# A planned attention-and-GLU kernel: transposing loads by whole chunks behind wv, the first q evicted by two engines, fill units that either half of TensorE may go on with, and all orders planned anew

## The chip, the cores and the metric

The kernel runs on one core of one Trainium2 chip. The metric is the device time of one execution in microseconds (us). Before the change the runs took 654.67 us in the median of three (654.21 to 656.93). The engines are called here as in the profile: PE (TensorE, with PEld for its weight loads), DVE (VectorE), ACT (ScalarE), POOL (GpSimd) and SP (SyncE, which only issues DMAs in this kernel).

## The reference

x is 2048 x 512 in bf16. One branch is attention with 32 heads of 16, without a mask; the other is a gated product of F = 1376 columns. A gate of one number for each row mixes them.

```python
def reference(A_x, A_wqkv, A_wo, B_x, B_w_gate, B_w_up, B_w_down, gate_w):
    x = A_x
    g = _sigmoid((x * gate_w).sum(-1, keepdims=True))
    # _A_ref: qkv = x @ wqkv, in 32 heads of Dh = 16
    scores = jnp.einsum("bhqd,bhkd->bhqk", q, k) * (Dh ** -0.5)
    p = _softmax(scores, axis=-1)
    a = (o of p @ v, heads side by side) @ wo
    # _B_ref
    b = ((x @ w_gate) * (x @ w_up)) @ w_down
    return g * a + (1 - g) * b
```

## The kernel before, in words

**Attention.** The queries are cut into 4 chunks of 512 rows, the heads into 4 blocks of 8, each in two sets of four (s): 32 groups of 4 heads x 512 queries, called quads, done one after the other. For each quad there are 16 steps, one for each 128 keys. TensorE is used as two row halves of 64 rows (r = 0, 1) with four column tiles of 32 each, and every PE operation of the main part (`pe64`) is four matmuls of 64 rows x 512 columns on one half. The two halves work beside each other. Both lie in one PE queue, whose order is fixed when the program is built; an operation of one half that depends on one of the other waits on a semaphore.

A step has four score operations (two on each half), which fill four PSUM banks. Then it goes one of two ways. In an A step ScalarE takes the exponential of the banks, one, two or three at a time (`exp`, L1863), and two P·V operations follow. In a D step DVE makes an approximate exponential by an integer trick (`dpass`, L1896), three shifted copies are made by DVE or GpSimd (`copy`, L1902 and L1903), and eight P·V operations follow. P·V accumulates in bank 7.

**Fill.** All the other matrix products are `_Unit`s: K, Q and V projections, the gate, the u and g products of the GLU, the output products. A unit has n operations on one half (phase 0) and then n on the other half (phase 1), into one bank, and is then evicted by DVE or ACT. They are called fill because they go where attention leaves PE free.

**The planner.** `_Sched` steps through time when the program is built, with costs for each operation, and writes down an order for each engine. At each moment it asks `try_pe`, `try_act`, `try_dve`, `try_pool`, `try_sp`. Which kind of work PE takes next is set by some fifty numbers (`PAR`), most of which are tables with one entry for each 2 us of planned time (`win`). `f_cont` goes on with a unit that was begun, `f_start` begins the next unit of the list `fill`, `f_slice` emits one operation of a unit. Only the orders and the waits that the data need go into the program; the planned times don't.

**The first stage.** `prologue` of `_Hw` (from L2064) is written out by hand. The first chunk of x is loaded in four parts by SP's and ACT's queues, transposed on PE with an identity, and multiplied with the first 128 columns of wq and wk: four products into bank 5 for q, and into banks 4 and 6 for K. q is evicted four times under four masks (`QM`): two by ACT (L2163, L2164), two by DVE (L2170, L2171). K goes out by DVE (L2162, L2165). The other three chunks of x come by transposing loads, four of 512 x 128 to a chunk, on SP's queue (L2071 is the helper `ld` that issues every load of the stage). wv is loaded by ACT's queue once wk and wq have landed. The planner takes over from there with times at which it expects these things (`t0`, `tx` for the chunks of x, `tw` for the weights); from `late0` on, eight loads with the other columns of wk and wq are issued on SP, `wgap` apart.

Of the kernel before, what the change touches and what calls it, by code (L numbers as in the profile page):

```python
# [110 lines left out]
class _Unit:  # L111
    __slots__ = ("name", "n", "slot", "need", "mm", "evac", "due", "ph", "half", "pos", "bank", "first", "okt", "lastop", "edur", "eeng", "eneed")

    def __init__(self, name, n, mm, need, evac, edur=0, slot=0.216, eeng="dve", eneed=()):
        self.name = name
        self.n = n
        self.mm = mm
        self.need = need
        self.evac = evac
        self.edur = edur  # L120
        self.slot = slot
        self.eeng = eeng
        self.eneed = eneed
        self.due = 0.0
        self.ph = 0
        self.half = 0
        self.pos = 0
        self.bank = None
        self.okt = 0.0
        self.lastop = None  # L130
        self.first = None
# [6 lines left out]
class _Sched:  # L138
# [380 lines left out]
    def late(self, i):  # L519
        if i < 8:  # L520
            key = {3: ("wk", True), 7: ("wq", True)}.get(i)
            self.dma(self.now, lambda: self.hw.late_load(i) if self.hw else None, 3.0, (lambda t, o: self.setr(key, t, o)) if key else (lambda t, o: None), 3)
            self.at(self.now + self.par["wgap"], lambda: self.late(i + 1))
# [86 lines left out]
    def f_slice(self, u, r):  # L610
        op = None
        i = u.pos
        start = u.ph == 0 and i == 0
# [7 lines left out]
        u.lastop = op  # L621
        u.pos += 1
# [3 lines left out]
        if u.pos == u.n:  # L626
            end = self.now + 0.385 + max(0.0, u.slot - 0.216)
            if u.ph == 0:
                u.ph, u.half, u.pos = 1, 1 - r, 0
# [3 lines left out]
            else:  # L633
# [7 lines left out]
                self.at(t)  # L641

# [33 lines left out]
    def f_start(self, r):  # L676
# [6 lines left out]
        u = self.fill[self.fnext]  # L683
        if not self.ok(u.need):
            return False
# [3 lines left out]
        self.fnext += 1  # L689
        u.bank = self.bank_get("F")  # L690
        u.half = r
        self.fact.append(u)
# [50 lines left out]
    def pe_phase(self, r):  # L743
# [26 lines left out]
        if self.o_avail <= self.now + 1e-9:  # L770
            n0, n1 = self.nready(vh), self.nready(1 - vh)
            busy = any(u.half == 1 - vh and 0 <= u.pos < u.n and not (u.ph == 1 and u.okt > self.now) for u in self.fact)
# [23 lines left out]
        if r != vh and self.g("v2") > 0 and self.v_job(r):  # L796
            return True
# [722 lines left out]
    def prologue(self):  # L1520
# [10 lines left out]
        self.act_v = t0 + 0.6  # L1531
        self.dve_v = t0 + 1.9
# [4 lines left out]
        self.setr(("k", 0, 0), t0 + 0.6, g("k"))  # L1537
        self.setr(("x0k",), t0, r["k"] + [r["q1"]] if self.hw else None)
        self.setr(("q", 0, 0, 0), t0, g("q"))
        self.setr(("q0b",), t0 + 0.6, g("q0b"))  # L1540
        self.setr(("q", 0, 0, 1), t0 + 2.0, g("q1"))
        self.setr(("qd", 0), t0 + 2.0, g("q1"))
# [18 lines left out]
        if self.hw:  # L1561
            self.clast[(0, 0)] = [r["od"]]
# [3 lines left out]
        self.at(t0 + 0.1, lambda: self.bfree.append(4))  # L1566
        self.at(t0 + 0.6, lambda: self.bfree.append(6))
        self.at(t0 + 2.0, lambda: self.bfree.append(5))
# [99 lines left out]
class _Hw:  # L1668
# [104 lines left out]
    def warm_mm(self, r):  # L1773
        lo, hi = 64 * r, 64 * r + 64
        mms = [(self.ps[32 * cc : 32 * cc + 32, 7, :], self.KT[lo:hi, 0, 0:32], self.QM[lo:hi, 0, 0, :], True, True, cc) for cc in range(4)]
        return self.pe64(r, mms, [self.r["k0"], self.r["q"]])
# [270 lines left out]
    def turn(self):  # L2047
        return self.P.op("pool", lambda g: g.tensor_tensor(self.mask[:], self.mask[:], self.mask[:], ALU.add), [self.r["q"], self.r["q0b"]])
# [15 lines left out]
    def prologue(self):  # L2064
# [11 lines left out]
        d_wk0 = ld("act", self.wk[:, :, 0:128], wcol(512, 640), "dwk0")  # L2076
# [21 lines left out]

        dT = []
        for ch in range(1, 4):  # L2100
# [54 lines left out]
        k0, kr, fq = proj(4, self.wk), proj(6, self.wk), proj(5, self.wq)  # L2155
        oq = None
        for t in range(4):
            oq = pex(lambda pe, t=t: fq(pe, t), [xe[t], d_wq0])
# [3 lines left out]
        e0 = dve(lambda v: v.tensor_copy(self.KT[:, 0, 0:128], self.ps[:, 4, 0:128]), [ok0])  # L2162
        q_a = P.op("act", lambda a: a.activation(self.QM[:, 0, 0, :], self.ps[:, 5, :], ACT.Copy, scale=self.mask[:, 0:1]), [oq, m1])  # L2163
        q_b = P.op("act", lambda a: a.activation(self.QM[:, 0, 2, :], self.ps[:, 5, :], ACT.Copy, scale=self.mask[:, 1:2]), [oq])  # L2164
# [3 lines left out]
        r["q"] = q_a  # L2168
        r["q0b"] = q_b
        q_c = dve(lambda v: v.tensor_scalar(self.QM[:, 0, 1, :], self.ps[:, 5, :], self.mask[:, 2:3], None, ALU.mult), [q_a, q_b])  # L2170
        r["q1"] = dve(lambda v: v.tensor_scalar(self.QM[:, 0, 3, :], self.ps[:, 5, :], self.mask[:, 3:4], None, ALU.mult), [q_c])  # L2171
        r["x0"] = xe[3]
        r["x0all"] = xe
        r["bankops"] = {0: [xe[0]], 1: [xe[1]], 2: [xe[2]], 3: [xe[3]], 4: [e0], 5: [q_c, r["q1"]], 6: [e1]}
        r["od"] = od
        r["ones"] = on
        r["er1"] = er1
# [381 lines left out]
```

## Time and profile before

| | |
|---|---|
| runs | 654.67 us median of 3, 654.21 to 656.93 |
| profiled execution, first to last instruction | 653.9 us, granted TensorE clock 1.000; no time around the span is given for it |
| instructions | 44031 |
| TensorE matmuls | 22842, some half of it busy 644.9 us |
| weight loads | 18026, 339.2 us |
| DVE, ACT, POOL busy | 609.7, 639.9, 534.8 us |
| DMA | 22.65 MB, 35 GB/s in the mean |
| chain that ended last | 94% of the span on PE, 3% on SP's queue, 1% on DMA, 1% on DVE |

The span is cut by engines in the page's first part; the stretches give the same for a part of the span, with the number of instructions that touch it in brackets. In the timeline a row is one instruction or several alike, with start and length; what stands in square brackets is how long the engine had been idle and what ended that. Records of ACT and DVE overlap a little with the next one of the same engine.

### The profile page before, as it was taken

Reading aid. Unit: us, or ns where it says so; the run is one execution under the profiler, and the core shown is the slowest. Engines: PE = TensorE matmul, PEld = TensorE weight load, DVE = VectorE, ACT = ScalarE, POOL = GpSimd, SP = SyncE. Lnnn points to the kernel's source line nnn. Section 1 sums busy time; section 2 is a strip of 40 time slices with the busy share of each in tenths; the row PEclk is TensorE's granted clock in tenths of the full one; section 3 lists DMA queues with packets and bytes.
Section 4 is the critical chain, followed back from the end, with each engine's and each line's share of the span. In section 5 each row is a group of like instructions: output and inputs, shape, how many; then the busy total and the mean of one; then the engine's idle time right before and its main releaser. Section 6 shows DMA issues by size and latency. Waiting matters only on the chain.

```text
span 653.9 us, 44031 instructions
## 1 busy us (share of the span) xinstructions
PE 644.9 (99%) x22842; PEld 339.2 (52%) x18026; DVE 609.7 (93%) x1001; ACT 639.9 (98%) x1001; POOL 534.8 (82%) x590
## 2 busy tenths in 40 slices
PE   8999999999999999999999999999999999999997
PEld 4464555555555545545554555555554555545552
DVE  7889999999998899999999999999999879999995
ACT  7999999999999999999999999999999999999996
POOL 1235889899999578899999798999998977997972
PEclk9999999999999999999999999999999999999999
DMA  7302342002110110101001010100101011010101
GB/s 156 76 13 61 89 110 35 9 12 70 52 42 9 33 33 16 35 5 35 8 20 31 18 41 13 41 10 13 29 8 43 13 30 38 5 44 8 30 7 49
DMA packets 34583, 22.65 MB, mean 35 GB/s; under 512 B 20028, under 2 KB 31132, under 8 KB 34400
## 3 DMA queue, kind: packets, MB, share of 16 engines
q1 hardware_dynamic: 32912, 18.80, 11.7%
q8 instruction: 159, 2.61, 1.7%
q10 hardware_dynamic: 1488, 1.05, 0.5%
q14 instruction: 24, 0.20, 0.1%
HBM read 11.71 MB, written 2.36 MB: 22 GB/s over the span
## 4 chain that ended last, share of the span: by engine, by line
PE 94%; SPq 3%; DVE 1%; DMA 1%; issue 0%; POOLq 0%; ACT 0%
PE ps L1756 75%; PE ps L1741 19%; SPq L2071 3%; DMA xT<-in_A_x_dram 1%; DVE DB L1896 1%; DVE OT L2061 0%; POOLq L88 0%; ACT oc L2033 0%; DVE KT L1911 0%; DVE hT L1937 0%; PE ps L2024 0%; POOLq L83 0%
## 5 line engine op out<-in xcount | busy, mean ns | idle before, releaser
L1756 PE MATMUL ps<-QM,KT 64*32 64x512 bf16 x6956 | 491.5, 377 | 1.5 <-DVE QM L2171 0.6
L1903 POOL INT64_ADD DB<-DB x433 | 400.0, 942 | 79.6 <-DVE DB L1896 33.3
L1863 ACT ACTIVATE PT<-ps 128x512 bf16<-128x512 f32 (+1 forms) x660 | 443.0, 814 | 0.7 <-PE ps L1756 0.3
L1896 DVE TENSOR_SCALAR DB<-ps 128x512 int16<-128x512 f32 (+1 forms) x623 | 404.8, 684 | 26.2 <-PE ps L1756 21.9
L1756 PEld LDWEIGHTS ps<-QM,KT 64*32 64x32 bf16 x6956 | 158.6, 90 | 179.9 <-DVE DB L1896 49.7
L1741 PE MATMUL ps<-DB,Vp 64*17 64x512 bf16 x3092 | 240.1, 376 | 0.0
L1756 PE MATMUL ps<-PT,Vp 64*17 64x512 bf16 x1798 | 201.9, 376 | 0.0
L1756 PE MATMUL ps<-DB,Vp 64*17 64x512 bf16 x1924 | 182.8, 376 | 0.0
L1741 PE MATMUL ps<-QM,KT 64*32 64x512 bf16 x1236 | 118.8, 376 | 0.1
L1756 PE MATMUL ps<-xT,wu 64*32 64x512 bf16 x1376 | 114.3, 377 | 0.0
L1863 ACT ACTIVATE xT<-ps 128x512 bf16<-128x512 f32 (+1 forms) x144 | 112.8, 856 | 0.4 <-PE ps L1756 0.4
L1756 PE MATMUL ps<-xT,wg 64*32 64x512 bf16 x1376 | 111.2, 376 | 0.0
L1756 PE MATMUL ps<-wd,hT 64*32 64x512 bf16 x1152 | 85.0, 376 | 0.0
L1756 PE MATMUL ps<-xT,Vp 64*17 64x512 bf16 x432 | 84.9, 376 | 0.0
L1863 ACT ACTIVATE wd<-ps 128x512 bf16<-128x512 f32 (+1 forms) x123 | 70.7, 702 | 0.3
L1756 PEld LDWEIGHTS ps<-PT,Vp 64*17 64x17 bf16 x1798 | 55.9, 87 | 18.2 <-issue 4.9
L1756 PEld LDWEIGHTS ps<-DB,Vp 64*17 64x17 bf16 x1924 | 46.5, 86 | 21.6 <-issue 1.7
L1903 POOL INT64_ADD DB<-wv x50 | 43.5, 888 | 7.4 <-DVE wv L1896 4.1
L1896 DVE TENSOR_SCALAR wv<-ps 128x512 int16<-128x512 f32 (+1 forms) x63 | 42.3, 692 | 1.8 <-PE ps L1756 1.1
L1756 PEld LDWEIGHTS ps<-xT,wg 64*32 64x32 bf16 x1376 | 34.4, 91 | 16.8 <-issue 2.9
L1756 PEld LDWEIGHTS ps<-xT,wu 64*32 64x32 bf16 x1376 | 34.3, 91 | 17.0 <-DVE DB L1896 1.7
L1903 POOL INT64_ADD wv<-DB x32 | 31.7, 992 | 9.1 <-DVE OT L2061 3.1
(112 smaller groups left out, 746.4 us busy)
## 6 DMA issues: line engine op xcount, KB each, us to landing
rb<-rscr SPq DMA_DIRECT2D x16, 256.0 KB
QM<-qraw SPq DMA_DIRECT2D x120, 16.0 KB, 2.3
oc<-oraw SPq DMA_DIRECT2D x60, 32.0 KB, 2.2
out_dram<-ost SPq DMA_DIRECT2D x12, 128.0 KB, 1.8
wd<-in_B_w_down_dram SPq DMA_DIRECT2D x10, 128.0 KB, 2.4
wu<-in_B_w_up_dram SPq DMA_DIRECT2D x12, 96.0 KB, 2.2
wg<-in_B_w_gate_dram SPq DMA_DIRECT2D x12, 96.0 KB, 2.3
wv<-in_A_wqkv_dram ACTq DMA_DIRECT2D x1, 512.0 KB, 4.5
```

The source lines that it names most:

```text
L1741: o = pe.add_instruction(mybir.InstMatmult(name=nc.get_next_instruction_name(), engine=mybir.EngineType.PE, ins=[pe.lower_ap(rhs), pe.lowe ...
L1756: o = pe.matmul(dst, lhs, rhs, start=st, stop=sp, tile_position=(64 * r, 32 * cc), skip_group_check=True)
L1863: return self.P.op("act", lambda a: a.activation(dst, src, ACT.Exp, scale=self.ES), deps)
L1896: return self.dve(lambda v: v.tensor_scalar(dst, src, self.YB, 0.0, ALU.add, ALU.max), deps)
L1903: return self.P.op("pool", lambda e: e.int64_add(o.bitcast(I64), a.bitcast(I64), 0x0001000100010001 * self.OFF[v]), deps)
L2071: return P.dma(eng, lambda e: e.dma_start(dst, src, **kw), deps, stream)
```

## The change

1. **Loads of the first stage.** The first part of wk goes from ACT's queue to SP's, behind wq. wv goes from ACT's queue to SP's, ahead of the transposing loads, and no longer waits for wk and wq. Each of the three later chunks of x is one transposing load of 512 x 512 in place of four of 512 x 128.
2. **First q and K.** q's products go to two banks (5 and 7), half of the 512 queries to each, and each of the four masked evictions is cut in two halves of 256. ACT makes the first half of two of them and the small K eviction; DVE makes the other six halves and the large K eviction. One memset of `QM` goes from DVE to POOL.
3. **Fill units.** `pos` of a unit is kept for each half. A new `f_steal` lets a half take over a unit that the other half has begun and left standing for 0.435 us of planned time; the unit's operations of this half are done then, and it is handed back later. Each change of half in a unit adds a wait of the one half's operation for the other's. `f_start` may begin a later unit when the next one's inputs aren't there yet (`fsel`).
4. **Orders.** The times that the planner expects in the first stage are new, and all tables: new orders for all engines. The work itself, the number of units and the choice of which keys may be D steps (`dks`) stay; how many D steps a quad makes follows from the new tables.

```diff
     def f_cont(self, r):
         for u in self.fact:
-            if u.half != r or u.pos >= u.n:
-                continue
-            if u.ph == 1 and u.okt > self.now + 1e-9:
+            if u.half != r or u.pos[r] >= u.n or u.okt > self.now + 1e-9:
                 continue
             self.f_slice(u, r)
             return True
         return False
 
+    def f_steal(self, r):
+        for u in self.fact:
+            if u.half != 1 - r or u.pos[r] >= u.n or u.okt > self.now + 1e-9 or u.last + 0.385 + 0.05 > self.now + 1e-9:
+                continue
+            u.half, u.okt = r, 0.0
+            self.f_slice(u, r)
+            return True
+        return False
+
     def f_slice(self, u, r):
...
-            if start:
+            if u.lasth is None:
                 deps = self.dep(u.need) + self.blast[u.bank]
-            elif i == 0:
+            elif u.lasth != r:
                 deps = [u.lastop]
-            op = self.hw.fill(u, r, i, start, u.ph == 1 and i == u.n - 1, deps)
...
+            op = self.hw.fill(u, r, i, u.lasth is None, i == u.n - 1 and u.pos[1 - r] == u.n, deps)
+        u.lastop, u.lasth = op, r
+        u.pos[r] += 1
+        u.last = self.now
...
@@ pe_phase
             if self.f_cont(r):
                 return True
+            if self.g("fsteal") > 1 and self.f_steal(r):
+                return True
             if debt >= -self.g("flead") and self.f_start(r):
                 return True
...
         if r != vh and self.g("v2") > 0 and self.v_job(r):
             return True
+        if self.g("fsteal") and self.f_steal(r):
+            return True
         return False
...
@@ prologue of _Hw
-        d_wk0 = ld("act", self.wk[:, :, 0:128], wcol(512, 640), "dwk0")
+        d_wk0 = ld("sp", self.wk[:, :, 0:128], wcol(512, 640), "dwk0")
...
+        r[("wv",)] = ld("sp", self.wv[:, :, :], wcol(1024, 1536), "dwv")
         dT = []
...
-                for kt in range(4):
-                    o = ld("sp", self.xT[:, ch, kt, :], self.x2[512 * ch : 512 * ch + 512, 128 * kt : 128 * kt + 128], "dxt%d" % ch, transpose=True)
+                o = ld("sp", self.xT[:, ch, :, :], self.x2[512 * ch : 512 * ch + 512, :], "dxt%d" % ch, transpose=True)
...
-        r[("wv",)] = ld("act", self.wv[:, :, :], wcol(1024, 1536), "dwv", [d_wk0, d_wq0])
-
-        qz2 = dve(lambda v: v.memset(self.QM[:, 1, 2:4, :], 0.0), [qz1])
+
+        qz2 = pool(lambda g: g.memset(self.QM[:, 1, 2:4, :], 0.0), [qz1])
...
-        q_a = P.op("act", lambda a: a.activation(self.QM[:, 0, 0, :], self.ps[:, 5, :], ACT.Copy, scale=self.mask[:, 0:1]), [oq, m1])
-        q_b = P.op("act", lambda a: a.activation(self.QM[:, 0, 2, :], self.ps[:, 5, :], ACT.Copy, scale=self.mask[:, 1:2]), [oq])
+        qa = [q_act(0, 0, [oq[1], m1])]
+        qb = [q_act(2, 0, [oq[1]])]
+        qa.append(q_dve(0, 1, [oq[3]]))
+        e0 = P.op("act", lambda a: a.activation(self.KT[:, 0, 0:128], self.ps[:, 4, 0:128], ACT.Copy), [ok0])
+        qb.append(q_dve(2, 1, [oq[3]]))
         e1 = dve(lambda v: v.tensor_copy(self.KT[:, 0, 128:512], self.ps[:, 6, 128:512]), [ok])
...
+        qc = [q_dve(1, i, [oq[2 * i + 1]] + qb) for i in (0, 1)]
+        r["q1"] = qc + [q_dve(3, i, []) for i in (0, 1)]
...
@@ PAR
- 'late0': 19.2,
+ 'late0': 14.1,
+ 'lgap': 0.75,
...
- 't0': 7.6,
- 'tw': [(('wk', False), 0), (('wq', False), 0), (('wv',), 10.5), (('gw',), 18.0)],
- 'tx': [6.4, 12, 16.5, 20.5],
+ 't0': 7.82,
+ 'tw': [(('wk', False), 0), (('wq', False), 0), (('wv',), 7.8), (('gw',), 17.6)],
+ 'tx': [6.6, 9.8, 13.9, 17.3],
```

The rest of the diff are the tables of `PAR` (all of those with an entry for each 2 us, and `fsteal` and `fsel` as two new ones), the start times that the planner takes from the new first stage (`p0`), and the second names for what `prologue` now returns as lists.

More of the change, by code (lines that the diff above doesn't have):

```diff
@@ L682, in f_start @@
             return False
-        u = self.fill[self.fnext]
-        if not self.ok(u.need):
-            return False
+        i = self.fnext
+        n = self.g("fsel") if self.fill[i].name[0] != "fin" else 0
+        while True:
+            u = self.fill[i]
+            if u.half is None and self.ok(u.need):
+                break
+            n -= u.half is None
+            i += 1
+            if n < 0 or i == len(self.fill) or self.fill[i].name[0] == "fin":
+                return False
         if u.name[0] == "fin":
@@ L688, in f_start @@
                 return False
-        self.fnext += 1
         u.bank = self.bank_get("F")
         u.half = r
+        while self.fnext < len(self.fill) and self.fill[self.fnext].half is not None:
+            self.fnext += 1
         self.fact.append(u)
@@ L771, in pe_phase @@
             n0, n1 = self.nready(vh), self.nready(1 - vh)
-            busy = any(u.half == 1 - vh and 0 <= u.pos < u.n and not (u.ph == 1 and u.okt > self.now) for u in self.fact)
+            busy = any(u.half == 1 - vh and u.pos[1 - vh] < u.n and not u.okt > self.now for u in self.fact)
             want = any(u.half == vh and u.ph == 1 for u in self.fact)
```

199 lines of the change are left out of this document (120 added, 79 removed), and 319 rows, old and new, of the table PAR.

## The prediction

> **What bounds the kernel now.** I read the page first (totals, shares of the chain), then the busy time by stretches (behind each stretch and its length: busy us and number of instructions of PE, weight loads, DVE, ACT and POOL, then the granted clock, the DMA engines' share and GB/s), then ScalarE's groups, and last the timeline of the first 25 us, where most of the edits lie.
>
> ```profile
> span 653.9 us, 44031 instructions
> ```
> ```profile
> PE 644.9 (99%) x22842; PEld 339.2 (52%) x18026; DVE 609.7 (93%) x1001; ACT 639.9 (98%) x1001; POOL 534.8 (82%) x590
> ```
> ```profile
> PE 94%; SPq 3%; DVE 1%; DMA 1%; issue 0%; POOLq 0%; ACT 0%
> ```
> ```profile
> 8.00:10.00 2.00, 1.57 (x31) 0.37 (x24) 1.77 (x3) 1.99 (x4) 0.18 (x1) 1.00 0.95 272
> 10.00:12.00 2.00, 1.54 (x44) 0.69 (x40) 1.99 (x4) 2.00 (x5) 0.00 (x0) 1.00 1.05 202
> 14.00:16.00 2.00, 2.00 (x88) 1.22 (x72) 1.54 (x3) 2.00 (x4) 1.96 (x2) 1.00 0.31 68
> 20.00:22.00 2.00, 1.61 (x64) 0.70 (x43) 1.40 (x4) 2.00 (x5) 0.00 (x0) 1.00 0.44 75
> 22.00:24.00 2.00, 0.83 (x32) 0.54 (x36) 0.50 (x1) 0.37 (x2) 0.00 (x0) 1.00 0.52 134
> 40.00:640.00 600.00, 599.11 (x21508) 314.87 (x16892) 569.70 (x919) 598.58 (x935) 524.98 (x572) 1.00 0.12 31
> ```
> ```profile
> 23.17 0.40 PE L1756 MATMUL ps<-xT,wk 64*32 64x512 bf16 x4 [1.56 <-DMA xT<-in_A_x_dram]
> 23.18 0.40 PE L1756 MATMUL ps<-wv,xT 64*32 64x512 bf16 x4
> 23.39 0.40 PE L1756 MATMUL ps<-xT,wk 64*32 64x512 bf16 x4
> ```
>
> The clock is 1.00 in all. PE is called busy while either of its two row halves runs, so 99% hides a half that stands still; the count of matmuls shows it. One half starts a group of four matmuls every 0.22 us (23.17 to 23.39; over several groups 0.216), so two halves can start 37 a microsecond. From 40 to 640 us 21508 matmuls need 581 us of PE: 19 us of 600 (3%) are idle halves. A full 2-us stretch counts 88 (74 starts and some 14 that it cuts). Against 88, the stretches from 8 to 12 us lack 101 matmuls (2.7 us) and those from 20 to 24 lack 80 (2.2 us).
>
> ```profile
> L1863 ACT ACTIVATE PT<-ps 128x1024 bf16<-128x1024 f32 x235 | 234.9, 1066 | 0.1
> L1863 ACT ACTIVATE PT<-ps 128x512 bf16<-128x512 f32 x423 | 227.7, 671 | 0.6 <-PE ps L1756 0.3
> L1863 ACT ACTIVATE xT<-ps 128x1024 bf16<-128x1024 f32 x72 | 73.5, 1053 | 0.4 <-PE ps L1756 0.4
> L1863 ACT ACTIVATE wd<-ps 128x512 bf16<-128x512 f32 x110 | 58.5, 661 | 0.2
> L1863 ACT ACTIVATE xT<-ps 128x512 bf16<-128x512 f32 x72 | 42.6, 659 | 0.0
> ```
> ```profile
> 23.86 0.60 ACT L1863 ACTIVATE wo<-ps 128x512 bf16<-128x512 f32 x1 [1.63 <-PE ps L1756]
> 24.36 1.08 ACT L1863 ACTIVATE hT<-ps 128x512 bf16<-128x512 f32 x2
> ```
> ```profile
> 353.29 1.04 ACT L1863 ACTIVATE xT<-ps 128x1024 bf16<-128x1024 f32 x1
> 354.19 1.05 ACT L1863 ACTIVATE PT<-ps 128x1024 bf16<-128x1024 f32 x1
> ```
> ```profile
> 644.36 1.08 ACT L1863 ACTIVATE xT<-ps 128x1024 bf16<-128x1024 f32 x1
> ```
>
> ScalarE is as full. Its records overlap, so I price them by their starts: two narrow exponentials (512 columns) took 1.08 us together and one 0.60, so they start 0.48 apart; wide ones (1024) start 0.90 apart, 353.29 to 354.19. The five groups hold 307 wide and 605 narrow ones: 276 + 290 = 566 us; the 89 other instructions at 0.48 or more add at least 43. That is 609 us; the last exponential ends at 645.4 and the first can't start before the first score, which a row below has at 8.19: at most 28 us of slack in 637 (4%). So PE and ScalarE are two nearly full resources, and the chain goes along PE only because they hand banks to each other. A step of attention can go over DVE in place of ScalarE: two wide exponentials (1.8 us) less for ScalarE, six more groups on PE (eight P·V groups for two), 6 x 0.216 / 2 = 0.65 us. New orders can thus turn idle PE halves into ScalarE relief, at 0.65 for 1.8.
>
> **The change, part by part.** The sum is against the profiled execution, 653.9 us; the median of the runs shown, 654.67, lies 0.8 above it, which I add at the end.
>
> ```profile
> 1.71 0.43 SPq L2071 DMA_DIRECT2D wq<-in_A_wqkv_dram  x1
> 2.19 17.39 SPq L2071 DMA_TRANSPOSE xT<-in_A_x_dram  x12
> ```
> ```profile
> 6.41 0.39 ACTq L2071 DMA_DIRECT2D wv<-in_A_wqkv_dram  x1
> 7.36 0.69 ACT L2163 ACTIVATE QM<-ps,mask 128x512 bf16<-128x512 f32 x1 [1.01 <-PE ps L2151]
> ```
> ```profile
> 7.10 1.06 PE L2151 MATMUL ps<-xT,wk 128*128 128x128 bf16 x16
> 8.19 0.41 PE L1756 MATMUL ps<-QM,KT 64*32 64x512 bf16 x8
> ```
> ```profile
> wv<-in_A_wqkv_dram ACTq DMA_DIRECT2D x1, 512.0 KB, 4.5
> ```
> ```profile
> wk<-in_A_wqkv_dram ACTq DMA_DIRECT2D x1, 128.0 KB, 4.7
> ```
> ```profile
> L2071 SPq DMA_TRANSPOSE xT<-in_A_x_dram x12: 1239/1262/2189, 2.2 to 18.3; - x12
> ```
> ```profile
> 18.32 4.72 DMA xT<-in_A_x_dram
> ```
> ```profile
> L2014 ACT ACTIVATE rb<-rb 128x256 f32<-128x256 f32 x2 | 0.8, 416 | 0.1
> ```
>
> *First wk to SP's queue.* It is issued behind wq, at 2.14, and with the same 4.7 lands at 6.8; K's matmuls start at 7.10, behind Q's. Cost 0. Without that cover (a landing 0.5 later still) the first score would be late by the excess; ends 0 to +0.4. What is queued behind it on SP goes one issue, about 0.43, later.
>
> *First q by two engines.* Four products of 512 (0.69 on ScalarE) become eight of 256 (0.42 by the nearest row): three on ScalarE's side with the small K eviction, six and the large K eviction on DVE. The first half can start when half of Q's matmuls are done, about 0.5 us before 7.36; the first score then waits for DVE's first half and the K eviction, both near 8.0 in place of 8.19. ScalarE is free sooner, DVE later: six at 0.42 are 2.5 us for two at about 0.69. I take -0.1; ends -0.5 and +0.5 (DVE's extra us, if its queue is what scores wait for). The memset of QM that moves from DVE to GpSimd lies in GpSimd's idle time, 0.18 us of the 4 from 8 to 12: 0.
>
> *wv ahead of the transposing loads.* It is issued at about 2.6 in place of 6.41; with the same 4.5 it lands near 7.1 instead of 10.9, and the V units of the first chunk (4 x 32 matmuls, 3.5 us at 37 a microsecond) can fill the 2.7-us hole from 8 to 12 us, in which ScalarE is busy throughout. It moves PE work and not ScalarE's, so only part of it shortens the span. Taken -0.5; ends 0 (DVE, 1.77 and 1.99 of 2 us busy there, has no time to evict V) and -2.0 (the hole times 0.74, PE's weight 1.8 / (1.8 + 0.65) in the exchange above).
>
> *Three transposing loads for twelve.* SP spent 17.4 us issuing twelve, 1.26 us each when undisturbed, and the last landed 4.72 us after its issue, at 23.04. PE's in-order queue stood 1.56 us behind a K unit for it, and ScalarE 1.63. No row shows a whole chunk in one load. Bounds: if it costs what four cost, wv's 0.39 and wk's 0.43 ahead of it on SP make the last landing 23.9, no gain; if it costs what a plain 512-KB load costs (4.5 us), three in a row from 3.0 on are there by 16.5 and the whole stall goes. From 14 to 16 us the DMA engines were 31% busy, so the issue and not the engines held the loads back: I am nearest to the second. Taken -1.6; ends 0 and -1.6. Next late would be ScalarE itself. gw and the eight late loads of wk and wq, behind them on SP, go earlier with them (the eight planned 0.75 us apart, not 1.2): no row of before has a wait for them, 0. wv's issue leaves ScalarE's queue, where it lay in the 1.01 us before the first q eviction: 0.
>
> [...]
>
> *Either half goes on with a fill unit, and new orders.*
>
> ```profile
> PEld ps L1756 <- DVE DB L1896: 56.7, 236, 0.7
> PEld ps L1756 <- ACT PT L1863: 40.9, 173, 0.7
> ```
> ```profile
> PEld ps L1756 <- PE ps L1756: 7.5, 34, 0.3
> ```
> ```profile
> 300.00:400.00 100.00, 100.00 (x3601) 52.88 (x2765) 97.20 (x159) 100.00 (x158) 90.57 (x106) 1.00 0.10 26
> 400.00:500.00 100.00, 100.00 (x3564) 51.94 (x2776) 96.82 (x158) 100.00 (x140) 92.95 (x97) 1.00 0.08 21
> ```
>
> It adds no matmul and no eviction; nor does starting a later unit where the next one's inputs aren't there, which goes with it. It adds a wait of one half for the other at every take-over, 0.22 us where it shows (7.5 / 34); queued behind it on PE are both halves' next groups, and their evictions on DVE and ScalarE. It can use the 19 us of idle halves. But the waits ahead of weight loads are mostly for banks that DVE and ScalarE have not emptied (56.7 and 40.9), which no stealing cures. I take a sixth of the 19 us, 3.3, at weight 0.74: -2.5. For the ends I use how far 100-us stretches of one and the same planner differ, 3564 to 3601 matmuls, 1% or 6 us over the span: new orders may land that far off on either side, -6 to +6. The sixth is a choice: the stretches show that 1% can be had, and a third of 19 us would be the -6 end's equal.
>
> Sum: 0 - 0.1 - 0.5 - 1.6 - 2.5 = -4.7, so 649.2 for an execution like the profiled one, and with the 0.8, **650.0 us**.
>
> **Rivals.** The runs shown spread over 2.7 us (654.21 to 656.93), so under 0.5%, 3.3 us, I call it no change.
>
> *A: only the first stage gains.* Bank waits stay what they are and the new orders are no denser: 654.67 - 2.2 = 652.5. For it: the two largest waits above are for evictions. Against: 3% of idle halves.
>
> *B, slower: the transposing loads land late.* PE's order is fixed, so a landing later than planned stops both halves, as at 21.6 to 23.17. The new plan awaits the chunks earlier (its settings put them 2.2 to 3.2 us sooner). If a whole chunk costs what four pieces did, the third lands at about 23.9, the stall of 1.6 grows by some 3 us and by the 0.8 of the two issues, and nothing else gains: 654.67 + 3.8 = 658.5. It decides as soon as the third landing lies past 23 us. Against it: the DMA engines' 31%.
>
> *C: hand-overs eat what they give.* Each take-over makes one half wait for the other. If there are as many again as show now, 34 waits of 0.22 cost 7.5 us of the weight loads' queue, half of it PE's: the -2.5 becomes +1.3, and 654.67 - 2.2 + 1.3 = 653.8. [...]
>
> **How the numbers follow.** Forecast (first stage and orders both gain, 645.0 at the lower ends to 651.4): 0.60. A: 0.19, C: 0.09, both within 0.5%. B: 0.08. Orders worse than that by themselves (the +6 end less 2.2 gives 658.5): 0.04. So faster 0.60, same 0.28, slower 0.12. The range runs from 644.5 (orders at -6 and wv at -2.0 give 645.0, the first score's lower end 0.4 less) to 657.0, which leaves out most of B and the worst orders. The likeliest case alone: 645 to 651.4.
>
> **What would show it.** wv's landing before 8 us and V matmuls from about 8.5 us; some 75 matmuls or more in 8:10 and 10:12; no wait of PE for xT and no 1.6-us gap on ScalarE; over 21600 matmuls in 40:640 or as many with a shorter span; more waits PE on PE, each near 0.2 us. Wrong would be: a stall for xT of over 3 us (B), a count in the middle that is unchanged (A), or PE-on-PE waits above 15 us in all (C).

## The result, and the profile after

The changed kernel takes 650.54 us (median of 9 runs, 649.52 to 651.98), the kernel before 654.13 beside it (9 runs, 652.59 to 656.93): ratio 0.9943, 95% interval 0.9929 to 0.9957, 3.6 us faster. The forecast was 650.0, with a range of 644.5 to 657.0.

The page of the kernel after, its totals and the shares of its chain:

```profile
span 648.7 us, 44347 instructions
```
```profile
PE 642.2 (99%) x22958; PEld 342.8 (53%) x18098; DVE 612.0 (94%) x1007; ACT 635.1 (98%) x1037; POOL 567.4 (87%) x646
```
```profile
PE 99%; issue 0%; POOLq 0%; ACT 0%; DVE 0%
```

The chain has lost SP's queue (3% before): no transposing load lies on it any more. The busy time by stretches of the kernel after (PE, weight loads, DVE, ACT, POOL, then clock, DMA share, GB/s):

```profile
8.00:10.00 2.00, 2.00 (x76) 1.12 (x73) 1.98 (x6) 1.48 (x3) 0.55 (x2) 1.00 1.09 225
10.00:12.00 2.00, 2.00 (x80) 1.12 (x68) 2.00 (x5) 1.97 (x5) 0.53 (x1) 1.00 1.98 226
12.00:14.00 2.00, 1.58 (x62) 0.79 (x46) 1.86 (x4) 1.83 (x4) 0.00 (x0) 1.00 0.76 146
16.00:18.00 2.00, 1.77 (x61) 0.75 (x40) 2.00 (x4) 1.95 (x5) 1.01 (x1) 1.00 0.48 139
18.00:20.00 2.00, 1.90 (x72) 1.11 (x64) 1.36 (x3) 1.45 (x4) 2.00 (x3) 1.00 0.51 148
20.00:22.00 2.00, 2.00 (x88) 0.98 (x52) 1.94 (x4) 2.00 (x5) 0.06 (x1) 1.00 0.01 4
22.00:24.00 2.00, 2.00 (x84) 0.97 (x60) 2.00 (x5) 2.00 (x5) 1.76 (x2) 1.00 0.03 8
40.00:640.00 600.00, 599.61 (x21712) 319.80 (x17057) 572.25 (x923) 598.79 (x967) 547.52 (x618) 1.00 0.12 31
```

The hole from 8 to 12 us is filled (156 matmuls for 75) and the one from 20 to 24 is gone (172 for 96). Between them something is lost again: the stretches 12:14, 16:18 and 18:20 have 62, 61 and 72 matmuls where before had 77, 84 and 88, together 54 fewer (1.5 us). From 40 to 640 us there are 204 more matmuls: by the prediction's own count, 37 started in a microsecond, 21712 need 587 us, so the idle halves fell from 19 to about 13 us of 600.

SP's queue and PE in the timeline of after:

```profile
2.74 0.51 SPq L2093 DMA_DIRECT2D wv<-in_A_wqkv_dram  x1
3.29 9.55 SPq L2093 DMA_TRANSPOSE xT<-in_A_x_dram  x3
```
```profile
8.04 0.40 PE L1778 MATMUL ps<-wv,xT 64*32 64x512 bf16 x4
```

Three issues of whole chunks hold SP for 9.55 us where twelve held it for 17.39, and V's products start at 8.04, beside the first score.

**Where the 3.6 us are.** The finished P·V bank of a quad is evicted by a product on DVE; for every other quad its row carries `oc<-ps,erow`. The first and the last of these 16 are two fixed points of the work. Nearly the same attention work lies up to, between and behind them in both kernels (scores of the next quad may run a little ahead, and a step may go over DVE or over ScalarE); fill can be moved across freely. From the answer for the tile `erow` (ns min/median/max, first and last start):

```profile
L1961 DVE TENSOR_TENSOR oc<-ps,erow x16: 678/680/692, 50.8 to 630.0; 128x512 f32<-128x512 f32 x16
```
```profile
L1983 DVE TENSOR_TENSOR oc<-ps,erow x16: 678/680/693, 49.8 to 624.0; 128x512 f32<-128x512 f32 x16
```

The first is of before, the second of after. So before needs 50.8 us to the first point, 579.2 between, 23.9 (653.9 - 630.0) behind; after 49.8, 574.2 and 24.7. The same three numbers of the other profiles, from the same row and the span of each:

| orders, loads | to the first | between | behind |
|---|---|---|---|
| before; twice more (e10, e11) | 50.8; 51.1, 50.2 | 579.2; 577.7, 578.3 | 23.9; 23.8, 23.9 |
| before's orders, new loads (e1, e2) | 49.7, 49.8 | 578.6, 578.4 | 23.9, 24.5 |
| after; its variants e4, e7, e9 | 49.8; 49.7, 49.6, 49.4 | 574.2; 574.7, 574.4, 574.7 | 24.7; 24.7, 24.8, 24.7 |
| after's orders, late loads (e3, e5, e6) | 52.8, 54.4, 53.7 | 575.4, 574.5, 574.4 | 24.9, 24.7, 24.8 |

Between the two points the old orders take 577.7 to 579.2 in five profiles, the new ones 574.2 to 575.4 in seven: 3.8 us less, whatever the loads. To the first point new loads are worth about 1 us with the old orders; with the new orders late loads cost 3 to 4.6. Behind the last point the new orders take 0.9 more (0.2 against e2). The stretches up to the first point, between the two and behind the last, of before and then of after, tell what was moved:

```profile
0.00:50.80 50.80, 46.68 (x1462) 27.05 (x1234) 41.59 (x81) 44.48 (x77) 14.08 (x23) 1.00 0.39 79
50.80:630.00 579.20, 578.31 (x20770) 303.64 (x16340) 551.16 (x890) 577.78 (x902) 511.14 (x555) 1.00 0.12 31
630.00:653.90 23.90, 19.91 (x628) 8.50 (x452) 16.97 (x32) 17.68 (x26) 9.62 (x14) 1.00 0.11 36
```
```profile
0.00:49.80 49.80, 47.78 (x1518) 26.50 (x1262) 45.14 (x90) 43.75 (x84) 25.54 (x36) 1.00 0.36 80
49.80:624.00 574.20, 573.81 (x20802) 306.10 (x16324) 551.39 (x891) 572.99 (x928) 531.95 (x602) 1.00 0.12 31
624.00:648.70 24.70, 20.62 (x664) 10.18 (x512) 15.47 (x30) 18.38 (x27) 9.91 (x11) 1.00 0.11 35
```

After does 56 matmuls more before the first point, in 1.0 us less, and 36 more behind the last (1.0 us at 37 a microsecond, about the 0.9). Sorted by their operands, 36 of the 56 are fill and 20 are scores, and behind the last point 44 more are fill. So some 80 matmuls of fill, 2 us of PE, have left the middle for the early holes and for the end. Yet the middle has not less to do on PE, but 32 matmuls more, since 120 more of P·V have come into it: it is shorter because it is denser. ScalarE is busy for all of it, 577.78 of 579.20 us before and 572.99 of 574.20 after: the middle lasts as long as ScalarE's work there, and that is 4.8 us less.

Where ScalarE's work went is seen in the groups of exponentials and in the whole count of matmuls. ScalarE's two main groups, after:

```profile
L1885 ACT ACTIVATE PT<-ps 128x512 bf16<-128x512 f32 x487 | 261.1, 660 | 0.6 <-PE ps L1778 0.5
L1885 ACT ACTIVATE PT<-ps 128x1024 bf16<-128x1024 f32 x208 | 208.9, 1062 | 0.2
```

The page counts 116 more matmuls than before (22958 - 22842), and the groups of DVE's approximate exponential take 740 banks in place of 720. That is five more steps that go over DVE, at six groups of four more for each on PE (120). They free ScalarE of 20 banks, ten wide exponentials, 9.0 us at 0.90. Something was given back, since wide exponentials were split: over all tiles wide ones went from 335 to 282 and narrow ones from 652 to 741, so some 43 wide ones became pairs, and each pair costs 0.06 more than a wide one, 2.6 us. The 6.4 us that remain by these prices are near the fall of ScalarE's busy time, 4.8 us (639.9 to 635.1 on the page). So idle halves of PE were exchanged for relief of ScalarE, which is still full (598.79 of 600). GpSimd, which makes copies for the D steps, is busy 32.6 us more. This account is read from counts; no run changes the number of D steps alone.

### The profile page after: what moved, and what is told of

Its sections match the earlier page's. It is cut to its first block, busy times and chain, and to the rows that moved or that the text cites. A ratio compares the mean times of both kernels' runs of the same rounds, so it can differ in the third digit from the quotient of the medians.

```text
span 648.7 us, 44347 instructions
## 1 busy us (share of the span) xinstructions
PE 642.2 (99%) x22958; PEld 342.8 (53%) x18098; DVE 612.0 (94%) x1007; ACT 635.1 (98%) x1037; POOL 567.4 (87%) x646
## 3 DMA queue, kind: packets, MB, share of 16 engines
q8 instruction: 160, 2.62, 1.6%
## 4 chain that ended last, share of the span: by engine, by line
PE 99%; issue 0%; POOLq 0%; ACT 0%; DVE 0%
PE ps L1778 78%; PE ps L1763 19%; PE ps L2146 0%; PE ps L2172 0%; PE ps L2155 0%; POOLq L88 0%; ACT oc L2055 0%; PE ps L2046 0%; PE ps L1820 0%; DVE PT L2102 0%; DVE warm L2101 0%; DVE mask L2105 0%; POOLq L83 0%
## 5 line engine op out<-in xcount | busy, mean ns | idle before, releaser
L1778 PE MATMUL ps<-QM,KT 64*32 64x512 bf16 x6988 | 499.8, 377 | 0.4 <-issue 0.4
L1925 POOL INT64_ADD DB<-DB x473 | 419.6, 906 | 51.0 <-DVE DB L1918 21.9
L1885 ACT ACTIVATE PT<-ps 128x512 bf16<-128x512 f32 (+1 forms) x696 | 449.6, 781 | 0.9 <-PE ps L1778 0.5
L1918 DVE TENSOR_SCALAR DB<-ps 128x512 int16<-128x512 f32 x635 | 414.5, 688 | 17.5 <-PE ps L1778 12.6
L1778 PEld LDWEIGHTS ps<-QM,KT 64*32 64x32 bf16 x6988 | 163.3, 90 | 173.4 <-DVE DB L1918 41.5
L1763 PE MATMUL ps<-DB,Vp 64*17 64x512 bf16 x3204 | 245.9, 376 | 0.0
L1778 PE MATMUL ps<-PT,Vp 64*17 64x512 bf16 x1812 | 203.3, 376 | 0.0
L1778 PE MATMUL ps<-DB,Vp 64*17 64x512 bf16 x1956 | 188.2, 377 | 0.0
L1763 PE MATMUL ps<-QM,KT 64*32 64x512 bf16 x1204 | 117.8, 376 | 0.0
L1778 PE MATMUL ps<-xT,wg 64*32 64x512 bf16 x1376 | 114.5, 377 | 0.4 <-issue 0.4
L1778 PE MATMUL ps<-xT,wu 64*32 64x512 bf16 x1376 | 111.9, 376 | 0.0
L1778 PE MATMUL ps<-wd,hT 64*32 64x512 bf16 x1152 | 87.5, 376 | 0.0
L1778 PE MATMUL ps<-xT,Vp 64*17 64x512 bf16 x420 | 84.3, 376 | 0.0
L1778 PEld LDWEIGHTS ps<-PT,Vp 64*17 64x17 bf16 x1812 | 56.6, 87 | 15.2 <-issue 2.5
L1885 ACT ACTIVATE wd<-ps 128x512 bf16<-128x512 f32 (+1 forms) x103 | 60.6, 696 | 0.1
L1778 PEld LDWEIGHTS ps<-DB,Vp 64*17 64x17 bf16 x1956 | 47.4, 86 | 20.4 <-issue 2.5
L1778 PEld LDWEIGHTS ps<-xT,wg 64*32 64x32 bf16 x1376 | 35.7, 91 | 17.9 <-PE ps L1778 1.9
L1778 PEld LDWEIGHTS ps<-xT,wu 64*32 64x32 bf16 x1376 | 35.3, 91 | 17.0 <-issue 2.4
L1925 POOL INT64_ADD DB<-wv x40 | 38.4, 980 | 1.0 <-PE ps L1778 0.7
L1778 PE MATMUL ps<-xT,wq 64*32 64x512 bf16 x480 | 38.6, 377 | 0.0
L1925 POOL INT64_ADD DB<-wk x41 | 35.0, 871 | 2.6 <-DVE DB L1924 2.3
```

What stands on the lines that cost most here:

```text
L1763: o = pe.add_instruction(mybir.InstMatmult(name=nc.get_next_instruction_name(), engine=mybir.EngineType.PE, ins=[pe.lower_ap(rhs), pe.lowe ...
L1778: o = pe.matmul(dst, lhs, rhs, start=st, stop=sp, tile_position=(64 * r, 32 * cc), skip_group_check=True)
L1885: return self.P.op("act", lambda a: a.activation(dst, src, ACT.Exp, scale=self.ES), deps)
L1918: return self.dve(lambda v: v.tensor_scalar(dst, src, self.YB, 0.0, ALU.add, ALU.max), deps)
L1925: return self.P.op("pool", lambda e: e.int64_add(o.bitcast(I64), a.bitcast(I64), 0x0001000100010001 * self.OFF[v]), deps)
```

## The experiments

The runs and their times; "before" is the kernel before, run beside them on the same chip.

| | kernel, us | before, us | ratio, 95% interval |
|---|---|---|---|
| e1 before's orders, new loads | 654.28 | 654.82 | 0.9993, 0.9982 to 1.0003 |
| e2 the same with the new first q | 654.36 | 654.82 | 0.9994, 0.9982 to 1.0005 |
| e3 after's orders, old loads | 654.52 | 654.82 | 0.9994, 0.9984 to 1.0005 |
| e4 after, late loads held back | 650.84 | 654.82 | 0.9937, 0.9924 to 0.9949 |
| e5 after, twelve small transposing loads | 654.95 | 654.11 | 1.0014, 1.0001 to 1.0027 |
| e6 after, wv on ACT's queue | 653.16 | 654.11 | 0.9985, 0.9970 to 1.0000 |
| e7 after, 275 more waits between halves | 650.15 | 654.11 | 0.9941, 0.9925 to 0.9957 |
| e9 after, transposing loads held for wq | 650.50 | 654.11 | 0.9944, 0.9932 to 0.9956 |
| e12 e6 with PE kept busy | 653.94 | 654.08 | 1.0004, 0.9994 to 1.0014 |
| e8 after without stealing, one run | 717.27 | 653.52 | |
| e10, e11 before, one run each | 654.36, 654.14 | 653.52 | |

**e1 and e2: the loads alone.** e1 is the kernel before with the new loads and its old orders on all compute engines; e2 is the code of after with before's tables and stealing off, so that PE's order is that of before and the first q is evicted in halves.

```diff
# e1, in before
-        d_wk0 = ld("act", self.wk[:, :, 0:128], wcol(512, 640), "dwk0")
+        d_wk0 = ld("sp", self.wk[:, :, 0:128], wcol(512, 640), "dwk0")
+        r[("wv",)] = ld("sp", self.wv[:, :, :], wcol(1024, 1536), "dwv")
-                for kt in range(4):
-                    o = ld("sp", self.xT[:, ch, kt, :], ..., transpose=True)
+                o = ld("sp", self.xT[:, ch, :, :], ..., transpose=True)
-        r[("wv",)] = ld("act", self.wv[:, :, :], wcol(1024, 1536), "dwv", [d_wk0, d_wq0])
# e2, in after: PAR of before, and
+PAR.update(fsteal=0, fsel=0)
```

> The orders of before for every compute engine, with the new loads alone (wk and wv on SP's queue, wv ahead, one transposing load for each chunk); q evicted as before. Theory (the first stage's gain is the stall for the third chunk, 1.56 us on PE and 1.63 on ACT, and wv's hole cannot be filled in a fixed order): 654.1 - 1.6 = 652.5, and no wait of PE for xT. Rival 1 (slack further on takes the 1.6 us up, the gain is all in the new orders): 654.1. Rival 2 (the loads are no faster but collide with PE's instruction fetch, two gaps of 0.8 us as in the kernel after): 653.5 to 655.

> The orders of before with the whole new first stage: the new loads, q evicted in halves by two engines, the memset on POOL. Theory: as the kernel with the loads alone, less 0.1 for the earlier first score: 652.4. Rival (DVE's six halves keep the first D step waiting, since DVE was busy from 8 to 12 us): 0.3 to 0.5 slower than with the loads alone.

Both come out at the time of before, 0.5 us below it with an interval that holds zero: the first rival was right (654.1, the gain is all in the orders), and the theory (652.5) was not. What e1's profile has from 8 to 12 us, and its only wait of PE for a load:

```profile
8.00:10.00 2.00, 1.67 (x33) 0.45 (x26) 1.67 (x3) 1.99 (x4) 0.18 (x1) 1.00 0.97 209
10.00:12.00 2.00, 1.65 (x44) 0.57 (x40) 2.00 (x4) 2.00 (x5) 0.00 (x0) 1.00 1.13 246
```
```profile
PE ps L2150 <- DMA wq<-in_A_wqkv_dram: 1.3, 1, 1.3
```

The stall for xT is gone, as expected, and yet only 0.5 is won. The hole stays, 33 and 44 matmuls, although wv is there from 8.5 us on: the old order has nothing else in that place. The wait for wq can't be put down to the new loads: e10, which is before unchanged, has 0.8 us of it. Of the 1.6 us that the prediction gave to this stall, most was never in the median; e10 and e11 say why.

**e10 and e11: before, unchanged, two more profiles.** To see how much of the 1.56-us stall of the first profile belongs to that one execution.

> The kernel before, unchanged, for another profile of the first stage. Theory (the third chunk's landing at 23.04 and the stall of 1.56 us in the first profile were a late draw, since the first profiled span, 653.9, is long beside the spans of other executions with the same surroundings): the third chunk lands at 20.5 to 22.5, the stall for it is under 1 us and the span 652.5 to 653.3. Rival (23.0 is the usual landing): a stall of 1.3 to 1.8 us again and a span near 653.9.

> As the run before it, a second profile: landing of the third chunk at 20.5 to 22.5 and a stall under 1 us by the theory, 23 us and 1.3 to 1.8 us by the rival.

In e11 PE's only wait for x is

```profile
PE ps L1756 <- DMA xT<-in_A_x_dram: 1.0, 1, 1.0
```

and in e10 there is none at all. The third chunk lands at 21.0 and 22.4 us there, against 23.04 in the first profile. The spans are 652.6 and 652.4 against 653.9: the execution I built the sum on was itself 1.3 and 1.5 us longer than its two repeats. e10 shows something else between 10 and 16 us, in the column of the granted clock:

```profile
10.00:12.00 2.00, 1.44 (x36) 0.66 (x36) 1.75 (x3) 1.80 (x3) 0.00 (x0) 0.84 1.11 215
12.00:14.00 2.00, 2.00 (x45) 1.24 (x36) 0.58 (x1) 1.18 (x2) 0.00 (x0) 0.50 0.82 82
14.00:16.00 2.00, 2.00 (x72) 1.29 (x52) 1.50 (x3) 1.50 (x2) 1.06 (x2) 0.81 0.31 68
```

Behind the hole TensorE ran some 3 us at half its clock, with 45 matmuls where e11 has 75. e12 comes back to it.

**e3: the new orders with the old loads.** The four load edits of e1 turned round, in after.

> The orders of the kernel after, with the loads of before (twelve transposing loads, wk and wv on ACT's queue, wv behind wk and wq). Theory: PE stands for wv until 10.9 in place of 8.0 (2.9 us) and then for the third chunk until about 23 (some 1.8 more), and all of it is lost: 650.5 + 4.7 = 655.2, slower than before. Rival (slack further on takes it up, the gain is in the orders): under 651.5.

```profile
PE ps L1778 <- DMA wv<-in_A_wqkv_dram: 3.0, 1, 3.0
```
```profile
8.00:10.00 2.00, 0.00 (x0) 0.00 (x0) 2.00 (x5) 0.00 (x0) 1.07 (x2) 1.00 1.17 284
10.00:12.00 2.00, 1.11 (x24) 0.94 (x28) 0.04 (x1) 0.36 (x1) 0.00 (x0) 0.77 1.13 182
12.00:14.00 2.00, 2.00 (x51) 1.38 (x36) 0.69 (x1) 1.17 (x3) 0.00 (x0) 0.50 0.93 81
```

The first wait and the stretches are of e3. 654.52: the whole gain is gone, though the middle is as short as that of after within 1.2 us (575.4). The new order puts a V unit ahead of the first score in PE's one queue; wv landing at 10.9 stops both halves. The 1.8 us for the third chunk that the theory added are not there. So neither part is worth anything measurable alone (loads -0.5, orders -0.3, both with an interval that holds zero) and both together are worth 3.6. The table of the three sections shows the sum behind it: orders give 3.8 in the middle and take 0.9 at the end, and without the loads they are some 2 us later at the first point than before is.

**e5 and e6: which load.** e5 puts back the twelve small transposing loads and keeps wv ahead of them; e6 keeps the three large ones and puts wv back on ACT's queue behind wk and wq.

```diff
# e5
-                o = ld("sp", self.xT[:, ch, :, :], ..., transpose=True)
+                for kt in range(4):
+                    o = ld("sp", self.xT[:, ch, kt, :], ..., transpose=True)
# e6
-        r[("wv",)] = ld("sp", self.wv[:, :, :], wcol(1024, 1536), "dwv")
+        r[("wv",)] = ld("act", self.wv[:, :, :], wcol(1024, 1536), "dwv", [d_wk0, d_wq0])
```

> The kernel after with twelve transposing loads of 512 x 128 in place of three, everything else (wv ahead on SP, the orders) kept. Theory: twelve issues of 1.26 to 1.45 us from 3.3 on and some 3 to 4.7 to land put the third chunk at 22; its K unit was begun at 18.3 in the kernel after, so PE stands some 4 us: 650.5 + 3.9 = 654.4. Rival (small loads usually land sooner than in the first profile of before, as the 20.8 of the kernel with the old loads suggests, and the stall is small): about 652.5.

> The kernel after with wv alone back on ACT's queue behind wk and wq, the three whole-chunk loads kept. Theory: the V units that open the fill list stand for wv until about 11, PE is stopped for 3.0 us at 8.0 as in the kernel with all old loads, nothing gives it back: 650.5 + 3.5 = 654.0. With the twelve small loads at 654.4 as well, the two are not added up: the wait for wv pushes the need for the third chunk back by as much. Rival (half of it is won back by idle halves later): 652.

The waits of PE for loads in e5, then its chain's last transfer, then the wait in e6:

```profile
PE ps L1778 <- DMA xT<-in_A_x_dram: 3.7, 2, 2.5
```
```profile
19.07 3.38 DMA xT<-in_A_x_dram
```
```profile
PE ps L1778 <- DMA wv<-in_A_wqkv_dram: 4.0, 1, 4.0
```

Each load by itself is needed: against after, e5 is 4.4 us longer and e6 2.6 (by the ratios to before, 4.6 and 2.7). e6 lies between its two forecasts. e5 shows the mechanism of rival B by other means: PE stands for a late third chunk, here with a landing at 22.45 us (19.07 + 3.38), short of the 23 that B named. And what the start loses is not won back: e5 is 4.6 us behind after at the first fixed point (54.4 and 49.8) and 4.9 at the last (628.9 and 624.0).

**e4 and e9: the smaller holes from 12 to 20 us.** After has two gaps in PE there that no wait explains, in the middle of a group of four:

```profile
13.71 0.39 PE L1778 MATMUL ps<-QM,KT 64*32 64x512 bf16 x2 [0.42 <-issue]
18.10 0.37 PE L1778 MATMUL ps<-wv,xT 64*32 64x512 bf16 x1 [0.33 <-issue]
```

A first theory was that PE's instructions come late because the eight late loads of wk and wq use the same engines at that time. (Instructions do come by DMA: the page of after has two queues of the kind `instruction`, 160 packets with 2.62 MB and 25 with 0.20, of which 4 and 1 fall in the first 26 us. That PE's come late was a guess.) e4 holds these back until 24 us (`late0` 24.0 in place of 14.1, and each waits for the latest PE operation); they are needed after 40 us only.

> The kernel after with the eight late loads of wk and wq issued from about 24 us on in place of 13.5; they are first used after 40 us. All else is the same. Theory (PE's gap of 0.8 us at 17.3 to 18.1, in the middle of a group and with no semaphore, is an instruction fetch that waits behind these loads): the gap goes, 650.5 - 0.7 = 649.8; the gap at 12.9 to 13.7 stays. Rival (the fetch waits behind the transposing loads, or the gap has another cause): 650.5 and both gaps stay.

e4's only row of this kind:

```profile
17.68 0.37 PE L1778 MATMUL ps<-wv,xT 64*32 64x512 bf16 x1 [0.54 <-issue]
```

The later gap stays with no late load under way, and the time is the same: that theory falls. (The earlier gap, which both forecasts kept, isn't in this profile.) e9 lets the first transposing load wait for wq, to give the plain loads ahead of it the engines alone (`[d_wq0] if ch == 1 else ()` in its issue).

> The kernel after with the first transposing load waiting until the first part of wq has landed (about 5.5 us in place of an issue at 3.3). Theory (the transposing loads slow the small loads of the first 8 us: PE waited 0.3 to 1.3 us for wq or 0.8 for wv in three of the five profiles with the new code): wq and wv land sooner and without a wait, the third chunk lands at about 17 and is needed at 18.1: 650.5 - 0.5 = 650.0. Rival (the third chunk is late): PE waits for xT for 1 us or more, 651.5.

No wait for wq or wv is left in e9, the transposing loads are issued 1.9 us later, and the time is 650.50. So the transposing loads have that to spare now, and neither the gain nor the loss that was put down came. Between 10 and 30 us only the profiles of after, e4, e7 and e9 have gaps of this kind, of 0.3 to 0.6 us; those of before and of the other variants (e1, e2, e3, e5, e6, e10, e11, e12) have none. They remain unexplained.

**e7: the price of a hand-over.** Rival C said that waits of one half for the other cost half of what they last. e7 adds one to each fill unit where an operation of the other half was planned at least 0.435 us earlier: 685 waits of PE on PE in the program that ran, for 410 (275 more; the expectation says 249).

```diff
+            elif i == 2:
+                x = next((o for t, o in reversed(self.hw.done[1 - r]) if t <= self.now - 0.435), None)
+                deps = [x] if x else []
```

> The kernel after with 249 more waits of one half of PE for the other (each fill unit's third operation on a half also waits for an operation of the other half that was planned at least 0.435 us before); before to after added 79. All orders stay. Rival C of the prediction (each wait costs 0.06 us of the weight loads' queue on average, half of that PE's, so 79 cost 2.4 us): 249 more cost 7.5 us, 658. Theory (the other half's matmuls cover most of it): at most 2 us, 650.5 to 652.5.

The waits ahead of weight loads, in after and then in e7 (its L1786 is after's L1778):

```profile
PEld ps L1778 <- DVE DB L1918: 46.3, 206, 0.5
PEld ps L1778 <- ACT PT L1885: 40.8, 175, 0.7
PEld ps L1778 <- PE ps L1778: 12.3, 53, 0.4
PEld ps L1778 <- PE ps L1763: 3.0, 12, 0.3
```
```profile
PEld ps L1786 <- PE ps L1786: 22.5, 96, 0.4
PEld ps L1786 <- PE ps L1771: 7.5, 32, 0.4
```

The waits double, 15.3 to 30.0 us, and the time is 650.15, no longer than that of after. PE itself is as busy as in after (641.3 and 642.2 us). So a wait in the row of weight loads is not by itself a price here. Rival C falls, and so does the bound of 15 us that the prediction gave for it: after reaches it and is faster.

**e8: no stealing.** After with `PAR.update(fsteal=0, fsel=0)` and all other tables as they are.

> The kernel after with taking over (fsteal) and choosing a later unit (fsel) switched off and all other tables as they are, so that the planner makes other orders. Theory (each entry of the tables fits the plan that it was found with, and once the first orders differ the rest no longer fits): far slower than before, 690 to 720, with many more matmuls missing in each stretch; so switching it off doesn't give its worth. Rival (the tables are general and the take-overs alone bring the gain): 652 to 655.

717.27, within what the theory put down. That would fit tables that suit only the plan for which they were chosen; the run says nothing about what stealing is worth. Whether the 3.8 us of the middle come from stealing or from a new search of the tables stays open: it would take tables searched for the code without stealing.

**e12: is the halved clock the cost?** e3, e5 and e6 have what e10 has: some 3 us at a clock of 0.50 behind their pause. Their executions all have a mean clock of 0.994 to 0.998 (31 of 31), while of the 26 of after, e4, e7 and e9 22 have 0.999 or more. e12 is e6 with matmuls, whose results are not read, put into the pause.

```diff
+        def keep_on(pe):
+            for i in range(34):
+                o = pe.matmul(self.ps[:, 1, 0:256], self.xT[:, 0, 0, 0:128], self.xT[:, 0, 0, 0:256], start=True, stop=True, skip_group_check=True)
+            return o
+        pex(keep_on, [xe[1], xe[3]])
```

> The kernel of e6 (whole-chunk loads, wv on ACT's queue and so late) with 34 matmuls of 128x256 whose result nobody reads, put on PE between the first K product and the first V unit, into a bank that is free then. At full clock they take some 3.6 us (0.107 each by the clock of 1.00 at which a 512-column matmul starts every 0.215) and lie in the 4.0 us that PE waited for wv in e6, where the granted clock was 0.50 from about 12.3 to 15.6 us afterwards. Theory (the halved clock behind the pause is a cost of its own): the clock stays 1.00 from 12 to 16 us, PE does some 70 to 80 matmuls a 2-us stretch there in place of 56, and of the 1.7 us so won about 0.74 reach the end: 651.9, ratio near 0.9967 against e6's 0.9985. Rival (only the wait for wv counts, the slow stretch is hidden by the evictions): the clock is mended and the time stays at e6's 653.2, ratio 0.9985. Against both: if the added matmuls hold the scores back, it is slower than e6.

e12's added work in the timeline, and the stretches behind it:

```profile
8.07 3.88 PE L2186 MATMUL ps<-xT 128*128 128x256 bf16 x34
```
```profile
12.00:14.00 2.00, 2.00 (x80) 1.10 (x68) 0.69 (x1) 1.64 (x4) 0.00 (x0) 1.00 1.92 204
14.00:16.00 2.00, 2.00 (x80) 1.15 (x60) 1.56 (x3) 1.97 (x4) 0.00 (x0) 1.00 0.64 94
```

The clock is mended (1.00, and a mean of 0.998 or more in all twelve runs) and the matmuls are as dense as was expected. The time is not shorter: ratio 1.0004 (0.9994 to 1.0014) against e6's 0.9985 (0.9970 to 1.0000). This doesn't settle what the halved clock costs, because the third outcome that was put down, that the added matmuls hold the scores back, is in the trace. wv's load and the first V unit of e12:

```profile
6.31 0.40 ACTq L2093 DMA_DIRECT2D wv<-in_A_wqkv_dram  x1
```
```profile
wv<-in_A_wqkv_dram ACTq DMA_DIRECT2D x1, 512.0 KB, 4.4
```
```profile
11.87 0.40 PE L1778 MATMUL ps<-wv,xT 64*32 64x512 bf16 x4
```

wv lands at 10.7 us (6.31 + 4.4), but the first V unit starts 1.2 us later, when the added matmuls are done, and the first score beside it. In e6's profile wv landed at 11.7 and the V unit started at once, at 11.70. From that start to the first fixed point e12 takes 40.8 us, e6 42.0 and e3 41.9. So in these profiles the slow stretch costs about 1.2 us, and e12 loses about as much ahead of it. One profile of each can't say what it costs in the median; that stays open, and would take added matmuls that end when wv lands. In before no cost shows: of its 70 runs beside the experiments 17 have a mean clock of 0.998 or less and 53 a higher one, and the median of both groups is 654.45.

## Why the prediction was right, and where it was not

*Total.* 650.0 was forecast and 650.54 measured, on the likely side of faster and by the main mechanism named: early holes closed, idle halves of PE turned into relief for ScalarE. That the number came within 0.6 is partly luck: the change was forecast at -4.7 and measured at -3.6, and half of that was made up by the kernel before, 654.67 in the median of three runs and 654.13 in that of nine. Two of the steps were mis-sized, in opposite directions, and so was the base.

*The base.* I put 0.8 on the span to get to the median. The device time of a profiled execution stands 1.8 above its span (650.46 and 648.7 for after, 654.36 and 652.6 for e10), so the first profile of before was, by estimate, an execution of about 655.7, a microsecond or more above its median (not every execution has these 1.8; e1's profile has 2.6). The sum ended at a span of 649.2, the profile has 648.7; with 1.8 in place of 0.8 the forecast would have been 651.0.

*wk to SP and first q by two engines: 0 and -0.1.* The first q is e2 against e1, 654.36 and 654.28: not measurable, as taken. wk's move is in both and was never run alone.

*Three transposing loads: -1.6.* This step failed in size. The stall was real, but one execution's: 1.56, 1.0 and none in three profiles of before. Removed with the old orders (e1) it is worth 0.5 in the median, interval -1.2 to +0.2. The bounds of 0 and -1.6 held. That a whole chunk costs more like one plain load than like four pieces held only in part: issues of 3.4 us in the median against 1.26 for a quarter, as the answer for line L2093 of after has it:

```profile
L2093 SPq DMA_TRANSPOSE xT<-in_A_x_dram x3: 1911/3362/4181, 3.3 to 9.5; - x3
```

The last landing is at 14.9, so 1.57 MB took 11.6 us from the first issue, 136 GB/s; the twelve small ones of e5 took 19.2 (3.30 to 22.45), 82 GB/s.

*wv ahead: -0.5.* The landing (before 8) and the counts (76 and 80) came as forecast. What I missed is that the load only helps an order that uses it (e1: 33 and 44), and that such an order needs it: 2.6 us are lost without it (e6). I priced the loads and the orders as terms that add; they are a condition of each other.

*New orders: -2.5.* Measured 3.8 in the middle less 0.9 behind it, 2.9, some of it by fill put into the early holes. The idle halves went from 19 to 13 us, a third and not the sixth that I took. (I called a third the equal of the -6 end; with the weight of 0.74 that I gave the sixth, it is -4.7.) And the -2.5 was forecast for the orders as such; without the new loads they are worth 0.3 (e3).

*Rivals.* A (only the first stage gains) is the opposite of what happened: most of it is in the middle. B did not come about, and e5 shows that its mechanism is real. C is refuted by e7: the waits that I priced at half their length cost nothing that can be measured there (30.0 us of them against 15.3), and the sign that I set for C, over 15 us of them, came (15.3) in a kernel that is faster.

## What to carry to other kernels

Cut a trace at fixed points of the work (the first and the last eviction of a kind), and compare the sections over several profiles: that separated 1 us at the start from 4 in the middle, which neither the chain nor the waits did. A stall read from one execution is a draw; look at how much its landing varies before it becomes a term of a sum. In a kernel whose orders are fixed when it is built, loads and orders aren't separate terms: try each alone and both together. Here neither was worth anything measurable without the other.

## What the runs showed of the hardware that was not expected

- In e3 a wait of 3.0 us of PE early in the program was followed by some 3 us at half the granted clock. Its stretches, one microsecond each:

```profile
11.00:12.00 1.00, 1.00 (x24) 0.82 (x24) 0.00 (x0) 0.36 (x1) 0.00 (x0) 0.53 0.92 197
12.00:13.00 1.00, 1.00 (x31) 0.63 (x16) 0.00 (x0) 0.73 (x2) 0.00 (x0) 0.50 0.38 83
13.00:14.00 1.00, 1.00 (x32) 0.74 (x20) 0.69 (x1) 0.45 (x1) 0.00 (x0) 0.50 1.48 79
14.00:15.00 1.00, 1.00 (x40) 0.82 (x28) 0.14 (x1) 0.64 (x2) 0.00 (x0) 0.76 0.90 103
```

  The same followed a pause of 2.5 us in e5 (granted clock 0.50 from 24 to 27 us), and in e10 no single pause over 0.8 us but a hole of several (0.50 from 12 to 14 us). By the rows of e3 the slow stretch lasted 3.4 us (0.94 + 1 + 1 + 0.48), an estimate that takes the clock as either full or half. What length of pause goes with it isn't shown: the first profile of before has a stall of 1.56 us and a like hole from 8 to 12 us (75 matmuls, 64 in e10), at 1.00 throughout.
- Waits of a weight load for the other row half cost nothing that can be measured here: 30.0 us of them in e7 against 15.3 in after, 650.15 against 650.54 us.
- How long the same loads take differs from run to run: the third chunk of before landed at 21.0, 22.4 and 23.0 us in three profiles, and PE waited none, 1.0 and 1.56 us for it (e10, e11 and the first).
